# A fused scan and MLP on one core: the second product with stationary weights and its result turned back by VectorE

## The chip, the core and the metric

The kernel runs on one core of a Trainium2 chip. The metric is the device time in microseconds of one execution on that core, lower is better. A core has TensorE (PE, matrix products; PEld is its loading of stationary operands), VectorE (DVE), ScalarE (ACT), GpSimd (POOL) and SyncE (SP), which issues most of the DMAs here. The engines run their own instruction lists in order and wait for one another by semaphores. PSUM, where TensorE writes, has eight banks of 512 float32 columns.

## The reference

Two steps follow each other. The first is a chunked scan over 768 tokens for 4 batches x 8 heads (head size 32, state size 16); its result is regrouped into 3072 rows of 256. The second is an MLP with a hard-swish between two products (256 to 2048 to 256).

```python
for c in range(nc):                       # scan, per chunk
    cum = np.cumsum(la, axis=-1)
    L = np.exp(cum[:, :, :, None] - cum[:, :, None, :]) * causal
    CB = np.einsum('bhin,bhjn->bhij', Cc, Bc)
    y_intra = np.einsum('bhij,bhjd->bhid', CB * L, xc)
    y_inter = np.einsum('bhin,bhnd->bhid', Cc, state) * np.exp(cum)[:, :, :, None]
    y[:, :, sl] = y_intra + y_inter
    Bx = np.einsum('bhjn,bhjd->bhjnd', Bc, xc) * decay_from_j[:, :, :, None, None]
    state = decay_full[:, :, None, None] * state + np.sum(Bx, axis=2)
...
x = attn_out.transpose(0, 2, 1, 3).reshape(B * S, H * D)
h = x @ w_in                              # [3072, 256] @ [256, 2048]
g = h * np.clip(h + 3.0, 0.0, 6.0) / 6.0
out = g @ w_out                           # [3072, 2048] @ [2048, 256]
```

The inputs are float64 where the generator leaves them so; the kernel decodes the two weight matrices on the chip at the start. All products are float32.

## The kernel before

The work is cut into six blocks of 128 token positions; a block holds those positions of all four batches, so 512 rows of the MLP. The loop variable `k` is the block whose MLP runs, `c = k + 1` the block whose scan is woven into it, and `ahead = k + 2` the block that is prepared. No scheduler decides: the order of calls in the source is the order on each engine (`tc.manual_schedule()`).

A block's MLP in blocks 1 to 5 has two stages. In the first, eight steps `s` each make two hidden slices of 128 (f = 2s and 2s + 1) by a Strassen-Winograd scheme with seven half-size products: `lead` (two products, then a copy `even` <- `odd` on ScalarE, L667, and a copy `up` <- `odd` on VectorE, L668), `early` (two), `middle` (two, then the adds L680 and L681 on VectorE) and `last` (one). `ramp` (L688, ScalarE) and `times_ramp` (L693, VectorE) make the activated slices in `gT`. `g_sums` (L752, GpSimd) adds quarters of gT for the second stage.

The second stage is `out_units`. It is again a seven-product scheme, run once for each half t of the tokens of a quarter. Stationary operand is a 128 x 128 piece of gT (or of its sums), moving operand a 128 x 128 piece of the weights `w4` or of their sums `wsums`; the result comes out with tokens on partitions, in the banks `oa` and `ob`, and VectorE adds the parts into `res` (L791 to L813). Four DMAs per block (L816) store it, 128 rows of 1 KB each.

The generator yields after each product, and between its steps the loop issues the scan of the block `c`: after step 2 `scores` (its parts: `from_state` L500, the products `cb` L522 and `into_state` L534, into the banks f0 to f3, y0 and y1) and `multiply` (ScalarE's copy L550, VectorE's four products L563 of L with cb, in the middle of which `new_state` L544 makes `mid`), then `renew`; after steps 2 to 5 `decay_ends` for the block `ahead` (32 exponentials on ScalarE, L385, eight for each batch, and the `bs` products L396 on GpSimd); after step 6 `results` (`mix` L588 with `from_state`, `keep` L602 on ScalarE, `sum_y` L649 on VectorE), `from_start`, and `rows`, which issues the loads of L and eto on SP; after step 9 `turn_all` (VectorE transposes L465 and what follows), where the block ahead is 3 or later (`TURN` is 3); after step 12 the `lead` of the next block. `load(ahead)`, which loads B, C and x of a block on SP, is issued at the first step of a block's first stage.

Tiles of one tag share a bank or buffer in turn: `ps` has one buffer for each of the tags f0 to f3, `ps_o` two for the tag o, `ps_y` one for each of y0 and y1. A tile of a tag can be written only when the readers of the one before it are done.

Of the kernel before, what the change touches and what calls it, by code (L numbers as in the profile page):

```python
# [8 lines left out]
FP32 = mybir.dt.float32  # L9
# [4 lines left out]
ALU = mybir.AluOpType  # L14
# [6 lines left out]
def kernel(  # L21
# [24 lines left out]
    nc = tc.nc  # L46
    P = 128
    NB, NH, S, D = x.shape
    N = B.shape[-1]
    DM, DF = moe_w_in.shape[0], moe_w_out.shape[0]  # L50
    NC = S // P
    TB = NB * P
# [5 lines left out]
    HT = P // 2  # L58
# [7 lines left out]
    ffn = ctx.enter_context(tc.tile_pool(name="ffn", bufs=1))  # L66
    ps = ctx.enter_context(tc.tile_pool(name="ps", bufs=1, space=PSUM))
    ps_o = ctx.enter_context(tc.tile_pool(name="ps_o", bufs=2, space=PSUM))
# [14 lines left out]
    TURN = 3  # L83
# [71 lines left out]
    def conceal_in(t, pattern):  # L155
# [24 lines left out]
        out=head, in_=head, pattern=[[-2 * N, NQ], [-N, 2]], compare_op=ALU.is_ge,  # L180
        fill=0.0, base=0, channel_multiplier=1)
    nc.gpsimd.affine_select(
        out=head, in_=head, pattern=[[2 * N, NQ], [N, 2]], compare_op=ALU.is_ge,
# [140 lines left out]
    ys, cbs, sps, adds = {}, {}, {}, {}  # L324
# [177 lines left out]
                    rhs=csT[pair, b, HALF[a]], start=(a == 0 and b == 0), stop=True,  # L502
                    tile_position=(32 * q, d0), skip_group_check=True)

    def scores(c):

        bT, cT, _ = bTs[c]
        cbs[c] = [ps.tile([P, NB, 2, HT], FP32, name="cb", tag=f"f{q}") for q in range(NQ)]
        both = [ps_y.tile([P, 2, NB, HT], FP32, name=f"y{u}", tag=f"y{u}") for u in range(2)]
        ys[c] = {(0, u): both[u][:, 0] for u in range(2)}
        sps[c] = [both[a if c else 1 - a][:, 1] for a in range(2)]
        if c:
            from_state(c, 0)
        for b in range(NB):
            for a, rows in enumerate(HALF):
                for q in range(NQ):  # L520
                    pair = slice(32 * q, 32 * q + 32)
                    nc.tensor.matmul(  # L522
                        out=cbs[c][q][rows, b], lhsT=bT[pair, b, rows],
                        rhs=cT[pair, b, :, rows], start=(b == 0), stop=True,
                        tile_position=(32 * q, a * HT), skip_group_check=True)
        into_state(c, 0, 1)

    def into_state(c, *halves):
        xt, bs = xts[c], bss[c]
        for b in range(NB):  # L530
            for q in range(NQ):
                hs = slice(b * NH + 2 * q, b * NH + 2 * q + 2)
                for a in halves:
                    nc.tensor.matmul(  # L534
                        out=sps[c][a][32 * q:32 * q + 32, b],
                        lhsT=bs[HALF[a], hs].rearrange("s h n -> s (h n)"),
                        rhs=xt[HALF[a], hs].rearrange("s h d -> s (h d)"),
                        start=(c == 0 and b == 0), stop=True, tile_position=(a * HT, 32 * q),
                        skip_group_check=True)
# [34 lines left out]
            op=ALU.mult)  # L574
        new_state(states[c], adds[c], later)

    def mix(c):


        xt = xts[c]  # L580
        ys[c].update({
            (1, u): ps.tile([P, NB, HT], FP32, name="y2", tag=f"f{u}") for u in range(2)})
        for u in range(2):
            for b in range(NB):
                for h in range(u * HU, (u + 1) * HU):
                    for a, rows in enumerate(HALF):
                        d0 = D * (h % HU)
                        nc.tensor.matmul(  # L588
                            out=ys[c][a, u][d0:d0 + D, b], lhsT=xt[rows, b * NH + h],
                            rhs=Ls[c][rows, b, h], start=(b == 0 and a >= min(c, 1)), stop=True,  # L590
                            tile_position=(a * HT, d0), skip_group_check=True)
            if c == 0:
                from_state(c, 1, (2 * u, 2 * u + 1))
        if c:
            from_state(c, 1)

    def keep(c):
# [24 lines left out]
    NJ = NF // 2  # L622
# [97 lines left out]
    w4 = w_out.rearrange("p (j e) (m c) -> p e m j c", e=2, m=2)  # L720
    wsums = {}
# [15 lines left out]
    gsums = {}  # L737

    def g_quarter(k, e, r):
        return gTs[k].rearrange("p (j e) (r i) -> p e r j i", e=2, r=2)[:, e, r]  # L740
# [13 lines left out]
    def out_units(k):  # L754
# [15 lines left out]
        for t in range(2):  # L770
# [47 lines left out]
                    in_=res[:, 2 * r:2 * r + 2].rearrange("p m c -> p (m c)"))  # L818
            yield

    def rows(c):
        load_decay(c)
        load_eto(c)

    def results(c):
        mix(c)
        keep(c)
        sum_y(c)

# [4 lines left out]
    def load(c):  # L834
        load_bc(c)
        load_x(c)

    parts = {i: decode(i) for i in range(2 * NP)}

    def weights(i, n):  # L840
        for _ in range(n):
            next(parts[i], None)
# [62 lines left out]
    for k in range(NC):  # L905
        gTs[k] = ffn.tile([P, NF, TB], FP32, name="gT")
        c, ahead = k + 1, k + 2
        if k == 0:
            for f in range(NF):
                mlp_in(k, f)  # L910
                for i in weave.get(f, []):
                    weights(i, 1)
                if f in (6, 8):
                    diff_exp(c, f // 2 - 3)
            load(ahead)
            weights(NP + 1, 1)
            weights(NP + 3, 1)
            weights(NP + 2, 3)
            sums, sums_in = weight_sums(), in_weight_sums()
            for i in range(NP):  # L920
                for b in range(NB):
                    first_out(b, i, c)
                    if (i, b) == (0, 0):
                        weights(NP + 3, 1)
                        weights(NP + 2, 1)
                        weights(NP + 3, 3)
                        rows(ahead)
                    elif (i, b) == (1, 0):
                        next(sums_in)
                        next(sums_in)  # L930
                    elif (i, b) == (2, 0):
                        turn(c, 1)
                        wake(c)
                        turn(c, 0)
                        for p in range(2):
                            conceal(ahead, p)
                    elif (i, b) == (2, 3):
                        scores(c)
                        multiply(c)
                        renew(c)  # L940
                        decay_ends(ahead, 0)
                        decay_ends(ahead, 1)
                        next(sums)
                    elif (i, b) == (3, 0):
                        next(sums)
                        decay_ends(ahead, 2)
                    elif (i, b) == (3, 1):
                        results(c)
                        next(sums)
                        decay_ends(ahead, 3)  # L950
                    elif (i, b) == (3, 3):
                        from_start(ahead)
            rows(ahead + 1)
            continue
        for s in range(NJ):
            early(k, s)
            if s == 0:
                if ahead < NC:
                    load(ahead)
                if c < NC:  # L960
                    carry(c)
            if s < NJ - 1:
                lead(k, s + 1)
            if s:
                last(k, s - 1)
                ramp(k, 2 * s - 2, evens[k, s - 1])
            middle(k, s)
            if s:
                times_ramp(k, 2 * s - 2, evens[k, s - 1])
            ramp(k, 2 * s + 1, odds[k, s])  # L970
            times_ramp(k, 2 * s + 1, odds[k, s])
            if s in (1, 3) and ahead < NC:
                conceal(ahead, s // 2)
            if s in (3, 5) and c < TURN:
                turn(c, s // 4)
            if s in (2, 4, 6):
                g_sums(k, s - 2)
        for i, _ in enumerate(out_units(k)):
            if i == 0:
                s = NJ - 1  # L980
                last(k, s)
                ramp(k, 2 * s, evens[k, s])
                times_ramp(k, 2 * s, evens[k, s])
                g_sums(k, s - 1)
                if k == 1:
                    next(sums)
            if c < NC:
                if i == 2:
                    scores(c)
                    multiply(c)  # L990
                    if c < NC - 1:
                        renew(c)
                if ahead < NC and 2 <= i < 6:
                    decay_ends(ahead, i - 2)
                if i == 6:
                    results(c)
                    if ahead < NC:
                        from_start(ahead)
                    if ahead + 1 < NC:
                        rows(ahead + 1)  # L1000
                if i == 9 and TURN <= ahead < NC:
                    turn_all(ahead)
                if i == 12:
                    lead(c, 0)
# [30 lines left out]
```

## Time and profile before

| | us |
|---|---|
| median of three runs (lowest, highest) | 359.74 (359.16, 359.88) |
| the profiled execution, its own time | 359.64 |
| its span from first to last instruction | 357.9 |
| TensorE busy | 347.9 (97%) |
| VectorE busy | 221.9 (62%) |
| ScalarE busy | 177.5 (50%) |
| GpSimd busy | 137.9 (39%) |
| start of the `lead` of block 2, 3, 4, 5 in the chain | 139.34, 194.07, 248.79, 303.26 |

In the lines of the profile, a group has its place in the source (L766), its engine, operation, output <- input, shapes and count, then busy time. In a timeline or in the chain, the first number is the start in us from the start of the span, the second the length. "PE" lines are TensorE's passes; a float32 matmul appears as two of them. The granted TensorE clock was 0.995 of full speed on the mean.

### The profile page before, as it was taken

How to read it: one execution, taken by the hardware profiler on the slowest of the kernel's cores; microseconds unless marked ns; L12 is line 12 of the kernel's file. 1: busy time of each engine (PE TensorE's matmuls, PEld its weight loads, DVE VectorE, ACT ScalarE, POOL GpSimd, SP SyncE). 2: the span in 40 equal slices, each digit the busy share in tenths (PEclk: the TensorE clock that was granted, in tenths of full speed). 3: DMA queues.
4: the chain of work that ended last, by engine and by line, in shares of the span. 5: the costliest groups of instructions: out<-in, count | busy, mean ns of one | idle time of the engine just before them, and what ended most of it. 6: DMA issues, size and time to landing. Idle time of an engine off the chain costs nothing.

```text
span 357.9 us, 9350 instructions
## 1 busy us (share of the span) xinstructions
PE 347.9 (97%) x3936; PEld 300.0 (84%) x3936; DVE 221.9 (62%) x426; ACT 177.5 (50%) x390; POOL 137.9 (39%) x139
## 2 busy tenths in 40 slices
PE   5799999999999999999999999999999999999996
PEld 2554458888888999888999888999888999888996
DVE  6599999975887463686444687434587431588111
ACT  4678887267763730674650575560576010476100
POOL 3300000362599521099522089610068600058700
PEclk9899999999999999999999999999999999999999
DMA  8979969502924061550043560001000000000000
GB/s 166 201 277 185 266 165 127 116 4 84 155 57 60 5 136 58 81 80 2 4 113 82 74 88 2 4 2 35 26 2 1 4 3 31 29 3 0 2 29 31
DMA packets 75482, 24.97 MB, mean 70 GB/s; under 512 B 66032, under 2 KB 71824, under 8 KB 74928
## 3 DMA queue, kind: packets, MB, share of 16 engines
q1 hardware_dynamic: 71056, 23.06, 33.9%
q10 hardware_dynamic: 4384, 1.31, 1.7%
q8 instruction: 31, 0.51, 0.6%
q14 instruction: 11, 0.09, 0.1%
HBM read 21.07 MB, written 3.29 MB: 68 GB/s over the span
## 4 chain that ended last, share of the span: by engine, by line
PE 91%; DVE 3%; DMA 3%; ACT 1%; SPq 1%; issue 0%; DVEq 0%; ACTq 0%
PE ob L766 18%; PE even L652 18%; PE oa L766 18%; PE odd L652 13%; PE o L707 8%; PE h L610 8%; PE y L588 3%; PE y L500 2%; PE cb L522 2%; DMA raw<-in_moe_w_in_dram 2%; DMA pairs<-in_C_dram 1%; PE y L534 1%; SPq L100 1%; DVE odd L681 0%; DVE up L668 0%
## 5 line engine op out<-in xcount | busy, mean ns | idle before, releaser
L752 POOL TENSOR_TENSOR s<-gT 128x512 f32<-128x512 f32 x20 | 26.4, 1318 | 89.7 <-DVE gT L693 89.7
L652 PE MATMUL even<-ts,w_sum 128*128 128x256 f32 x160 | 48.2, 383 | 0.0
L667 ACT COPY even<-odd 128x512 f32<-128x512 f32 x40 | 23.0, 576 | 48.6 <-PE odd L652 46.3
L688 ACT ACTIVATE gT<-odd,half 128x512 f32<-128x512 f32 x40 | 27.5, 688 | 34.9 <-DVE odd L681 34.9
L652 PE MATMUL odd<-yT,w_in 128*128 128x256 f32 x160 | 41.1, 379 | 0.0
L766 PE MATMUL oa<-w_out,gT 128*128 128x128 f32 x320 | 38.9, 277 | 0.0
L766 PEld LDWEIGHTS oa<-w_out,gT 128*128 128x128 f32 x320 | 38.1, 192 | 0.9
L766 PE MATMUL ob<-w_out,s 128*128 128x128 f32 x320 | 37.4, 275 | 0.0
L766 PEld LDWEIGHTS ob<-w_out,s 128*128 128x128 f32 x320 | 36.5, 192 | 0.0
L652 PEld LDWEIGHTS even<-ts,w_sum 128*128 128x128 f32 x160 | 29.9, 190 | 5.3 <-ACT up L674 1.5
L693 DVE SCALAR_TENSOR_TENSOR gT<-gT,odd 128x512 f32<-128x512 f32 x40 | 27.5, 688 | 9.9 <-ACT gT L688 9.9
L652 PEld LDWEIGHTS odd<-yT,w_in 128*128 128x128 f32 x160 | 30.1, 190 | 3.9
L385 ACT ACTIVATE L<-L,cum_n 128x64 f32<-128x64 f32 x128 | 31.1, 339 | 0.0
L766 PE MATMUL ob<-t,gT 128*128 128x128 f32 x240 | 30.3, 279 | 0.0
L688 ACT ACTIVATE gT<-even,half 128x512 f32<-128x512 f32 x40 | 27.8, 695 | 4.4 <-PE even L652 4.4
L693 DVE SCALAR_TENSOR_TENSOR gT<-gT,even 128x512 f32<-128x512 f32 x40 | 27.2, 680 | 4.4 <-ACT gT L688 4.4
L766 PEld LDWEIGHTS ob<-t,gT 128*128 128x128 f32 x240 | 27.9, 192 | 1.2 <-issue 0.5
L707 PE MATMUL o<-w_out,gT 128*128 128x256 f32 x128 | 28.7, 381 | 0.0
L668 DVE COPY up<-odd 128x256 f32<-128x256 f32 x40 | 17.0, 424 | 18.6 <-ACT even L667 17.9
L610 PE MATMUL h<-yT,w_in 128*128 128x512 f32 x64 | 27.7, 594 | 0.0
L707 PEld LDWEIGHTS o<-w_out,gT 128*128 128x128 f32 x128 | 24.1, 190 | 3.7 <-issue 0.5
L563 DVE TENSOR_TENSOR L<-L,cb 128x512 f32<-128x512 f32 x24 | 15.3, 681 | 18.0 <-PE cb L522 15.5
(130 smaller groups left out, 609.8 us busy)
## 6 DMA issues: line engine op xcount, KB each, us to landing
raw<-in_moe_w_out_dram SPq DMA_DIRECT2D x4, 1024.0 KB
L<-cum_d SPq DMA_DIRECT2D x8, 512.0 KB
xt<-in_x_dram SPq DMA_DIRECT2D x6, 512.0 KB
raw<-in_moe_w_in_dram SPq DMA_DIRECT2D x3, 1024.0 KB
out_dram<-res SPq DMA_DIRECT2D x20, 128.0 KB
eto<-cum_e SPq DMA_DIRECT2D x20, 64.0 KB
B<-in_B_dram SPq DMA_DIRECT2D x5, 256.0 KB
raw<-in_moe_w_in_dram ACTq DMA_DIRECT2D x1, 1024.0 KB
```

Of the source, the lines that this page charges most:

```text
L385: nc.scalar.activation(Ls[c][:, b, h], Ls[c][:, b, h], AF.Exp, bias=cum_n[:, c, g:g + 1])
L563: nc.vector.tensor_tensor(out=Ls[c][:, :, hs], in0=Ls[c][:, :, hs], in1=cbs[c][q], op=ALU.mult)
L588: nc.tensor.matmul(out=ys[c][a, u][d0:d0 + D, b], lhsT=xt[rows, b * NH + h], rhs=Ls[c][rows, b, h], start=(b == 0 and a >= min(c, 1)), sto ...
L610: nc.tensor.matmul(out=h.rearrange("p r i -> p (r i)"), lhsT=w_in[:, j, f * P:(f + 1) * P], rhs=yTs[k][:, j].rearrange("p b i -> p (b i)") ...
L652: nc.tensor.matmul(out=bank[:, r], lhsT=lhsT, rhs=rhs, start=start, stop=True, skip_group_check=True)
L667: nc.scalar.copy(out=even, in_=odd[:, 1:2].to_broadcast([P, 2, 2 * P]))
L668: nc.vector.tensor_copy(out=up[:, 1], in_=odd[:, 0])
L688: nc.scalar.activation(gTs[k][:, f], h.rearrange("p r i -> p (r i)"), AF.Relu, bias=half, scale=1.0 / 6.0)
L693: nc.vector.scalar_tensor_tensor(out=g, in0=g, scalar=1.0, in1=h.rearrange("p r i -> p (r i)"), op0=ALU.min, op1=ALU.mult)
L707: nc.tensor.matmul(out=o[:, b % 2], lhsT=gTs[0][:, f, b * P:(b + 1) * P], rhs=w_out[:, f], start=(f == 0 and b % 2 == 0), stop=True, skip_ ...
L752: nc.gpsimd.tensor_tensor(out=o, in0=p_, in1=q_, op=op)
L766: nc.tensor.matmul(out=bank[:, slot], lhsT=lhs[:, j], rhs=rhs[:, j], start=(clear and j == 0), stop=True, skip_group_check=True)
```

## The change

In blocks 1 to 4 the second stage is made by a new generator, `wide_units`, while block 5 keeps `out_units` and block 0 its own form. The weights (or their sums) become the stationary operand, and a quarter of gT with 256 token columns is the moving one. A product is then eight matmuls of 256 columns, and there are seven products, each yielding twice, after four matmuls each. The result has output columns on partitions and tokens along the free dimension. VectorE transposes it in 32 x 32 squares (`turned_back`), and 32 DMAs per block store it, each 32 partitions of four runs of 32 floats.

The two `ps_o` banks `oa` and `ob` are taken once per block; a third bank, `oc`, is taken from tag f2 between the scan's use of that bank and the next block's. Two copies are made by ScalarE (`res`, `third`) and one by VectorE (`u2`).

The scan's parts move in two blocks. In block 2 (where c is TURN) `mix` issues its first half after step 6 and its second half after step 7, with `keep`, `sum_y` and what follows `results`. In block 4 (where c is NC - 1) `scores` leaves out `into_state`, which is issued after step 3, followed there by `multiply`.

```diff
-    def scores(c):
+    def scores(c, sums=True):
...
-        into_state(c, 0, 1)
+        if sums:
+            into_state(c, 0, 1)
...
-    def mix(c):
+    def mix(c, parts=range(2)):
...
-        for u in range(2):
+        for u in parts:
...
-        if c:
+        if c and 1 in parts:
             from_state(c, 1)
...
+    def wide_units(k):
+        halves = [[g_quarter(k, e, r) for r in range(2)] for e in range(2)]
+        g2, g4, g1 = (gsums[k][n] for n in (2, 4, 1))
+        def product(bank, slot, lhs, rhs, js, clear=False):
+            for j in js:
+                nc.tensor.matmul(
+                    out=bank[:, slot], lhsT=lhs[:, j], rhs=rhs[:, j],
+                    start=(clear and j == 0), stop=True, skip_group_check=True)
+        near, far = range(NJ // 2), range(NJ // 2, NJ)
+        res = ffn.tile([P, 2, 2, 2 * P], FP32, name="wide")
+        back = ffn.tile([P, 2, TB], FP32, name="back")
+        def turned_back(m, r=None):
...
+            nc.vector.transpose(out=o, in_=i)
+        def store(m):
+            for b in range(NB):
+                r0 = b * S + k * P
+                for q in range(4):
+                    c0 = m * P + 32 * q
+                    nc.sync.dma_start(
+                        out=out[r0:r0 + P, c0:c0 + 32].rearrange("(c i) m -> i c m", i=32),
+                        in_=back[32 * q:32 * q + 32, m, b * P:(b + 1) * P].rearrange(
+                            "i (c m) -> i c m", m=32))
+        oa, ob = (ps_o.tile([P, 2, 2 * P], FP32, name=n, tag="o") for n in ("wa", "wb"))
+        product(oa, 0, w4[:, 0, 0], halves[0][0], near, clear=True)
+        yield
+        product(oa, 0, w4[:, 0, 0], halves[0][0], far[:-1])
+        yield
+        product(ob, 0, wsums[4], halves[1][1], near, clear=True)
+        yield
+        product(ob, 0, wsums[4], halves[1][1], far)
+        yield
+        oc = ps.tile([P, 2, 2 * P], FP32, name="wc", tag="f2")
+        product(oc, 0, w4[:, 1, 0], halves[1][0], near, clear=True)
+        yield
+        product(oc, 0, w4[:, 1, 0], halves[1][0], far)
+        product(oa, 0, w4[:, 0, 0], halves[0][0], far[-1:])
+        nc.scalar.copy(out=res[:, 0, 0], in_=oc[:, 0])
+        nc.vector.tensor_tensor(out=res[:, 0, 0], in0=oa[:, 0], in1=res[:, 0, 0], op=ALU.add)
+        yield
+        product(oc, 1, wsums[3], halves[0][1], near)
+        yield
+        product(oc, 1, wsums[3], halves[0][1], far)
+        third, u2 = (ffn.tile([P, 1, 2 * P], FP32, name=n) for n in ("third", "u2"))
+        nc.scalar.copy(out=third, in_=oc[:, 1:2])
+        turned_back(0, 0)
+        yield
+        product(ob, 1, wsums[1], g1, near)
+        yield
+        product(ob, 1, wsums[1], g1, far)
+        nc.vector.tensor_tensor(
+            out=res[:, :, 1], in0=ob, in1=third.to_broadcast([P, 2, 2 * P]), op=ALU.add)
+        yield
+        product(oa, 0, wsums[2], g2, near)
+        yield
+        product(oa, 0, wsums[2], g2, far)
+        nc.vector.tensor_copy(out=u2, in_=oa[:, 0:1])
+        nc.vector.tensor_tensor(
+            out=res[:, :, 1], in0=res[:, :, 1], in1=u2.to_broadcast([P, 2, 2 * P]), op=ALU.add)
+        turned_back(0, 1)
+        store(0)
+        yield
+        product(ob, 1, w4[:, 1, 1], g4, near)
+        yield
+        product(ob, 1, w4[:, 1, 1], g4, far)
+        nc.vector.tensor_tensor(out=res[:, 1, 0], in0=ob[:, 1], in1=u2[:, 0], op=ALU.add)
+        turned_back(1)
+        store(1)
+        yield
...
-        for i, _ in enumerate(out_units(k)):
+        for i, _ in enumerate((wide_units if c < NC else out_units)(k)):
...
                 if i == 2:
-                    scores(c)
+                    scores(c, c < NC - 1)
+                if i == (2 if c < NC - 1 else 3):
+                    if i == 3:
+                        into_state(c, 0, 1)
                     multiply(c)
...
-                if i == 6:
-                    results(c)
+                if i == 6 and c == TURN:
+                    mix(c, (0,))
+                if i == (7 if c == TURN else 6):
+                    results(c, (1,) if c == TURN else range(2))
```

In the changed program, the lines after the new text move: L563 becomes L564, L668 L670, L680 L682, and the matmul of `product` is L832.

## The prediction

> **What bounds the kernel now.** I read the busy shares and the chain first, then the chain stage by stage in blocks 1 to 5 (blocks are k in the code; 0 is the first), then the timelines of the engines around each product stage.
>
> ```profile
> PE 347.9 (97%) x3936; PEld 300.0 (84%) x3936; DVE 221.9 (62%) x426; ACT 177.5 (50%) x390; POOL 137.9 (39%) x139
> PE 91%; DVE 3%; DMA 3%; ACT 1%; SPq 1%; issue 0%; DVEq 0%; ACTq 0%
> 153.28 1.29 PE even L652 x6
> ```
>
> TensorE is the bound: 97% busy, 91% of the chain. So only two things count: the rate of its passes, and what it waits for. The last line gives the rate of a pass that streams 256 columns: 1.29 / 6 = 0.2157 us (14 passes, 148.37 to 151.39 in the timeline, give the same). Each float32 matmul shows as two passes. This is the product stage of block 3 in the chain:
>
> ```profile
> 219.88 1.72 PE oa L766 x14
> 221.60 0.43 PE even L652 x2
> 222.04 3.79 PE oa L766 x34
> ...
> 227.43 0.79 PE y L534 x53
> 228.22 1.98 PE ob L766 x16
> 230.20 1.79 PE oa L766 x16
> 231.99 3.57 PE ob L766 x32
> ...
> 237.62 1.98 PE ob L766 x16
> 239.60 1.79 PE oa L766 x16
> 241.39 0.02 issue
> 241.41 2.02 PE ob L766 x16
> ```
>
> A pass of 128 columns is 3.57 / 32 = 0.1116 us. Where a group takes more, TensorE waited. The first 14 passes should take 1.56 and take 1.72: their last weights are gT of f = 12, which VectorE ends at 220.38 + 0.68 = 221.06. Each 1.98 is 0.19 over 1.79: it follows small-tile work (y, cb), and 0.19 is the price of one such visit, in and out. The 2.02 is 0.23 over: the second ob takes a bank that VectorE's L813 still reads, as this shows:
>
> ```profile
> 240.98 0.28 DVE L813 TENSOR_TENSOR res<-ob,u 128x128 f32<-128x128 f32 x1
> ...
> 241.38 1.86 PEld L766 LDWEIGHTS ob<-t,gT 128*128 128x128 f32 x16 [0.18 <-issue]
> ```
>
> The 2.02 is there in blocks 1 to 3, not in 4 (1.79 at 296.11).
>
> **The passes.** Before, a block's second product is 112 matmuls, 224 narrow passes: 224 x 0.1116 = 25.00. After, 7 products x 8 matmuls x 2 = 112 wide passes: 112 x 0.2157 = 24.16. Gain 0.84 per block; four blocks change (block 5 keeps the old form), so 3.36. Here a rule is to be weighed. TensorE: Matmul & The Clock Gate, section Back-to-back issue gap, says that in a stream of load-and-multiply pairs a 128-column matmul takes about 81 ns against 56 alone, so that loading costs some 25 ns each. The change drops 112 loads per block; at 25 ns this would be 11.2 us. The row decides: two narrow passes cost 223.2 ns, one wide 215.7, so a dropped load is worth 7.5 ns. Loads are hidden here.
>
> **Waits that go.** The 0.16 for f = 12: j = 6 now comes after 8 wide passes, the last even (0.43) and 4 more passes, 3.0 us in, not 1.3. Gain 0.16 in each of four blocks. The 0.23 for the ob bank: no second ob is taken. Gain 0.23 in blocks 1 to 3.
>
> **Waits that come.** I traced each bank through the instruction order of the changed program with its waits.
>
> (a) The first matmul of the product into slot 1 of the new bank oc is listed with a wait on ScalarE. The one ScalarE instruction it can be is the copy of oc slot 0: the bank is guarded as a whole. So a bank does wait for a copy, against the words of the change. And ScalarE's order puts that copy behind 24 of the 32 decay exponentials (blocks 1 to 3). Their rows:
>
> ```profile
> 228.28 0.37 ACT L550 COPY adds<-y 128x256 f32<-128x256 f32 x1 [2.04 <-PE y L534]
> 228.55 7.75 ACT L385 ACTIVATE L<-L,cum_n 128x64 f32<-128x64 f32 x32
> ```
>
> They start 0.33 after the end of into_state (228.22), at a pitch of (7.75 - 0.34) / 31 = 0.239. So the copy starts at +0.33 + 24 x 0.239 = +6.07, ends at +6.44 (0.37 as L550), and TensorE restarts at +6.60 (0.05 for the signal; 0.11 for an exposed load: the even at 218.20, held by DVE odd, lasts 0.70 where free ones last 0.59). Without it, TensorE would be there at 0.19 + 3 x 1.726 (8 passes each: ob far, oc near, oc far) + 0.43 = +5.80. Wait: 0.80 in each of blocks 1 to 3. Queued behind the copy are eight exponentials, then the copies of y; they have until the next block. In block 4 no exponentials run: the copy ends 0.41 after oc far, the two covering oa passes last 0.43, and 0.14 is left. Bounds for (a): 0.14 (ScalarE free) and 1.2 (one more copy-length late); I take 0.80, from the very rows.
>
> (b) oc needs the bank f2, which L563 for q = 2 reads. Blocks 1 to 3: cb ends at 227.43, and the second pair of L563 starts at 229.21, so q = 2 ends 229.21 + 0.68, 1.67 after into_state; TensorE comes at 0.19 + 1.73 = 1.92. No wait. In block 4, though, into_state is moved behind ob far, and VectorE's order is L, L, mid, mid, L, L with mid waiting for into_state. The rows of before, block 4:
>
> ```profile
> 282.21 1.28 DVE L563 TENSOR_TENSOR L<-L,cb 128x512 f32<-128x512 f32 x2 [4.01 <-PE cb L522]
> 283.42 0.60 DVE L544 SCALAR_TENSOR_TENSOR mid<-y,parity,tmp 128x128 f32<-128x128 f32 x2
> 283.94 1.27 DVE L563 TENSOR_TENSOR L<-L,cb 128x512 f32<-128x512 f32 x2
> ```
>
> Mid starts 0.07 after into_state, q = 2 ends 0.52 + 0.68 later, TensorE restarts 0.16 later: 1.43 during which it has nothing else. This is my value; ends 0.2 (a mere extra visit) and 1.7.
>
> (c) Block 2 splits mix around oc far: one more visit, 0.19 (ends 0 and 0.4, from the 1.98 rows). The steps of results move with its second part: the y copies, sum_y, from_start, and on SP two L and four eto loads. SP takes 1.85 + 2.50 for them in block 2 (182.37, 184.33); their readers are conceal (POOL) and carry in the next block, over 15 us later: nothing.
>
> (d) VectorE per block: out go L791 x2, L801, L802, L807, L811, L812, L813, 3.1 us; in come two adds of 256 (0.43 each), two of 512 (0.68), a copy (0.42), and transposes of 256, 256, 512. L465's row says 1.10 for 512; half for 256 is my estimate (0.55; ends 0.55 and 1.10). Sum 4.8, that is 1.7 more. ScalarE: two copies for one, 0.37. Neither bounds. What TensorE needs from them: the oa refill waits for an add done about 10 us before; the ob refill waits for the 512 add, done about 2.5 us before. At the block's end an add and the long transpose stand before L668, L680 and L681: see the rivals. Nothing.
>
> (e) Stores: 32 of 16 KB in 128-byte runs replace 4 per block. DMA: Bandwidth & Descriptors, Specifications, speaks against it: below 512 B a transfer is read, modified and written. Packets of this trace take 33.9% x 16 x 357.9 / 71056 = 27 ns, 4096 packets over 16 engines 7.0 us per block; doubled by the rule, 14 us. The DMA share is 0.33, 0.22 and 0.03 in blocks 2 to 4, so either fits. On SP:
>
> ```profile
> 204.20 4.54 SPq L100 DMA_DIRECT2D pairs<-in_B_dram  x8
> ```
>
> 0.57 each, 32 make 18 us. Behind them wait load(ahead): B, 16 pairs and x. B is then issued some 15 us later than at 197.59, its reader (bs, POOL) comes at 230.65 in block 3; the pairs' reader at 241.18. Cost nothing; no gain either, since no store is on the chain before block 5.
>
> **The sum.** Blocks 1 and 3: 0.84 + 0.16 + 0.23 - 0.80 = +0.43 each. Block 2: 0.43 - 0.19 = +0.24. Block 4: 0.84 + 0.16 - 0.14 - 1.43 = -0.57. Together 0.53 faster. Against the profiled execution, 359.64 (span 357.9 and 1.74 around it): 359.1. The median, 359.74, stands 0.10 above it, so 359.2.
>
> **Rivals.** A difference under 0.2% (0.72 us) can't be told from none here.
>
> 1. My sum, 359.2, with its small terms each off by 0.2: 358.6 to 359.8. Chance 0.55, of which 0.22 lie below 359.02.
> 2. The ScalarE wait is mostly not paid: with 0.14 instead of 0.80 in three blocks, 357.2. For it: before, ScalarE has idle time in this stage; against: the exponentials ran without a gap for 7.75. Chance 0.12.
> 3. Loads are worth the rule's 25 ns: 11.2 instead of 3.36, 351.4. Against: the 0.1116 row. 0.03.
> 4. The block's end becomes VectorE's. After the last product it has the 256 add (0.43) and the 512 transpose (1.10), 1.73 with the signal. L668 waits until 2.53 after that point today (253.81 against 251.28), L681 ends at 3.83, and TensorE needs it for the last even product at 4.38 (146.21 against 141.83 in block 2). So 0.8 + 0.5 = 1.3 us of slack. If the transpose or a late add eats more, TensorE waits in all four blocks: late by 1.75 us costs 0.45 each, 1.8 in all, and 361.0. It decides against the change (above 360.46) from 1.6 us on. For it: the slack is short; against: seven transposes in a narrow 1.08 to 1.11. 0.15.
> 5. The copy waits and visits are a little dearer and eat the gain: 359.7 to 360.6, 0.15.
>
> Faster 0.22 + 0.12 + 0.03 = 0.37; slower 0.15 + 0.03 of case 5's tail = 0.18; same 0.45. The range 357.8 to 360.8 leaves out case 3, most of 2 and the end of 4.
>
> **What would show it.** L832 at 0.2157 per pass; in blocks 1 to 3 a TensorE wait of about 0.8 on ScalarE's copy (L872) after the lone oa pass pair; in block 4 about 1.3 on L564 before the first oc pass; no wait at the ob refill; L668 and L682 no later against the first even product than now. A longer product stage in blocks 1 and 3, or a VectorE wait at a block's start, would prove me wrong.

## The result and the profile after

| | before | after |
|---|---|---|
| median of 22 runs each, us | 360.07 | 360.69 |
| profiled execution, its own time | 359.64 | 361.07 |
| its span | 357.9 | 359.3 |
| product stage of block 1, 2, 3, 4 | 29.13, 28.91, 28.91, 28.65 | 28.69, 29.05, 29.18, 30.22 |

The changed kernel takes 1.0023 of the time before, with an interval of 1.0001 to 1.0046; in a second comparison it took 1.0025 (1.0000 to 1.0051). That is some 0.8 us slower, where 0.5 us faster was forecast. (An execution's time goes with its mean granted clock, for the changed kernel 360.3 us at 0.997 or more, 361.6 at 0.99 and 364.9 at 0.98, and "at full clock" means those at 0.997 or more alone.) At full clock the difference is 0.9 to 1.2 us (before: 359.4 and 359.2 in two later comparisons), and between the two profiled executions it is 1.4. A product stage here runs from the first `oa` or `wa` of a block to the first product of the next block, in the chain; the half product that follows it takes 0.06 us less after, in every block. From here on, "the stage" means this.

The page of the changed kernel, first part and instruction refills (the queue's packets, MB, share):

```profile
PE 345.2 (96%) x3488; PEld 282.5 (79%) x3488; DVE 227.7 (63%) x426; ACT 178.7 (50%) x394; POOL 138.1 (38%) x139
q8 instruction: 27, 0.44, 0.5%
```

TensorE has 448 passes fewer and is busy 2.7 us less, and yet the span is 1.4 us longer: the difference is 4.1 us more of idle TensorE. The waits of TensorE say where (engine, line, what it waited for: us in total, times, longest):

```profile
PE wc L832 <- ACT wide L872: 1.9, 3, 0.6
PE wc L832 <- DVE L L564: 1.4, 1, 1.4
PE y L590 <- issue: 0.5, 2, 0.3
```

None of the three is in the list of before. The first two are the forecast ones, (a) and (b). The forecast had named 0.8 for each wait on L872, and 0.63 is listed; the other 0.24 of the cost is in the eight passes that follow each wait, which take 1.97 where eight undisturbed ones take 1.73. The third was not forecast: "issue" means that TensorE waited for nothing the profile shows, and L590 is `mix`. The chain of the changed kernel through the stage of block 3:

```profile
224.75 0.55 PE y L500 x25
225.37 0.98 PE cb L522 x55
226.35 0.83 PE y L535 x53
227.47 5.84 ACT L L385 x24
233.71 1.97 PE wc L832 x8
235.67 1.40 PE y L590 x89
237.56 0.62 PE y L500 x32
238.19 1.92 PE wc L832 x8
240.11 3.45 PE wb L832 x16
```

3.45 / 16 = 0.2157 us is the wide pass, as priced. From into_state's end the chain passes through 24 exponentials of ScalarE (L385) and on to the second `wc`. And `mix` (L590) has 1.89 us to the start of L500 (237.56 - 235.67), where in block 3 before it took 1.44 (235.56 to 237.00). The timeline of TensorE's passes there, and then that of its loads:

```profile
236.28 0.79 PE L590 MATMUL y<-L,xt 64*32 64x64 f32 x58
237.32 0.24 PE L590 MATMUL y<-L,xt 64*32 64x64 f32 x1 [0.26 <-issue]
237.49 0.69 PE L500 MATMUL y<-csT,mid 32*64 32x64 f32 x32
...
237.32 0.10 PEld L590 LDWEIGHTS y<-L,xt 64*32 64x32 f32 x1 [0.42 <-issue]
```

The very last of 128 small passes starts 0.46 us after the one before it, and its load is late too. Block 4, in the chain:

```profile
281.28 1.92 PE wb L832 x8
283.21 0.83 PE y L535 x53
284.10 0.61 DVE mid L545 x2
284.71 0.60 DVE L L564
285.44 3.69 PE wc L832 x16
289.69 1.97 PE wc L832 x8
291.65 1.07 PE y L590 x70
293.00 0.54 PE y L590 x35
293.54 0.62 PE y L500 x32
```

VectorE's `mid` waits for the moved `into_state`, L564 waits for `mid`, TensorE waits for L564: 1.40 us from 284.04 to 285.44. And `mix` pauses here too, between 70 and 35 recorded passes. The stage of block 3 is longer than before (29.18 against 28.91), which the prediction had named as a sign that it is wrong.

### The profile page after: what moved, and what is told of

It is laid out like the page before. It is cut to its first block, busy times and chain, and to the rows that moved or that the text cites. A ratio compares the mean times of both kernels' runs of the same rounds, so it can differ in the third digit from the quotient of the medians.

```text
span 359.3 us, 8565 instructions
## 1 busy us (share of the span) xinstructions
PE 345.2 (96%) x3488; PEld 282.5 (79%) x3488; DVE 227.7 (63%) x426; ACT 178.7 (50%) x394; POOL 138.1 (38%) x139
## 3 DMA queue, kind: packets, MB, share of 16 engines
q1 hardware_dynamic: 87184, 23.06, 35.5%
## 4 chain that ended last, share of the span: by engine, by line
PE 85%; ACT 6%; DVE 4%; DMA 3%; issue 1%; SPq 1%; DVEq 0%; ACTq 0%
PE even L654 18%; PE odd L654 13%; PE wb L832 10%; PE o L709 8%; PE h L612 8%; PE wa L832 7%; PE wc L832 5%; ACT L L385 5%; PE oa L768 4%; PE ob L768 3%; PE y L590 3%; PE cb L522 2%; PE y L500 2%; DMA raw<-in_moe_w_in_dram 2%; PE y L535 1%; DMA pairs<-in_C_dram 1%
## 5 line engine op out<-in xcount | busy, mean ns | idle before, releaser
L385 ACT ACTIVATE L<-L,cum_n 128x64 f32<-128x64 f32 x128 | 31.4, 339 | 0.0
L690 ACT ACTIVATE gT<-even,half 128x512 f32<-128x512 f32 x40 | 27.8, 695 | 4.4 <-PE even L654 4.4
L832 PE MATMUL wb<-s,w_out 128*128 128x256 f32 x128 | 29.7, 380 | 0.0
L403 POOL TENSOR_TENSOR tmp<-state,eto 128x256 f32<-128x256 f32 x5 | 3.4, 683 | 64.0 <-DMA eto<-cum_e 51.6
L670 DVE COPY up<-odd 128x256 f32<-128x256 f32 x40 | 17.0, 424 | 16.6 <-ACT even L669 15.7
L832 PEld LDWEIGHTS wb<-s,w_out 128*128 128x128 f32 x128 | 24.2, 190 | 3.3
L754 POOL TENSOR_TENSOR s<-s,gT 128x512 f32<-128x512 f32 x20 | 25.5, 1274 | 1.6
L754 POOL TENSOR_TENSOR gT<-gT 128x512 f32<-128x512 f32 x20 | 25.5, 1274 | 0.0
L754 POOL TENSOR_TENSOR s<-gT,s 128x512 f32<-128x512 f32 x20 | 25.4, 1272 | 0.0
L564 DVE TENSOR_TENSOR L<-L,cb 128x512 f32<-128x512 f32 x24 | 15.3, 680 | 14.9 <-PE cb L522 13.2
```

Of the source, the lines that this page charges most:

```text
L385: nc.scalar.activation(Ls[c][:, b, h], Ls[c][:, b, h], AF.Exp, bias=cum_n[:, c, g:g + 1])
L564: nc.vector.tensor_tensor(out=Ls[c][:, :, hs], in0=Ls[c][:, :, hs], in1=cbs[c][q], op=ALU.mult)
L670: nc.vector.tensor_copy(out=up[:, 1], in_=odd[:, 0])
L690: nc.scalar.activation(gTs[k][:, f], h.rearrange("p r i -> p (r i)"), AF.Relu, bias=half, scale=1.0 / 6.0)
L754: nc.gpsimd.tensor_tensor(out=o, in0=p_, in1=q_, op=op)
L832: nc.tensor.matmul(out=bank[:, slot], lhsT=lhs[:, j], rhs=rhs[:, j], start=(clear and j == 0), stop=True, skip_group_check=True)
```

## The experiments

**Pauses and refills.** The instruction queue q8 moves packets of 16 KB, 27 in this kernel, 31 before. TensorE's recorded instructions are 2 x 3488 (a load and a pass each): 6976 / 256 = 27.3, and before 7872 / 256 = 30.8. So q8 is taken for TensorE's list, one packet for 256 instructions. I numbered TensorE's loads and passes in each trace, and looked for the pauses that no wait explains and the packet that began before each. All pauses that no wait explains, from block 1 on and over 0.15 us, in five of the kernels (the last three are those of experiments 1, 3 and 5); the 0.19 that every start of `into_state` shows and the 0.13 that a block's first `wc` product loses, wherever they fall, are left out. Experiments 2 and 7 have no such pause.

| kernel | block, place | number of the instruction | above a multiple of 256 | us after a q8 packet began |
|---|---|---|---|---|
| before | 1, from_state | 2994 | 178 | 2.4 |
| after | 3, mix | 5038 | 174 | 2.4 |
| after | 4, mix | 6058 | 170 | 2.4 |
| scan undivided | 2, after from_state | 4016 | 176 | 2.4 |
| scan undivided | 3, mix | 5038 | 174 | 2.7 |
| scan undivided | 4, after into_state | 5804 | 172 | 2.8 |
| scan undivided | 4, mix | 6058 | 170 | 2.3 |
| both edits | 2, after from_state | 4018 | 178 | 2.4 |
| both edits | 4, after into_state | 5808 | 176 | 2.8 |
| both edits, shifted by 64 | 1, after from_state | 2996 | 180 | 2.4 |
| both edits, shifted by 64 | 3, after into_state | 4784 | 176 | 2.3 |

Every pause ends at the same place in a 256-instruction grid, and 2.3 to 2.8 us after a refill began. Block 0 has one more in some executions, at number 700, 188 above a multiple: none in the changed kernel's first profile, 0.91 us in its second, 0.75 in experiment 1. So whole times of one kernel can differ by nearly 1 us from this alone, and the stages are the finer measure. The clock is not behind the pauses: in all four stages of both kernels the granted clock is 1.00. Small-tile runs use up the list fastest: mix's 256 instructions take 1.44 us, in which wide passes use 13.

**1. The scan in one piece again.**

```diff
-                    scores(c, c < NC - 1)
-                if i == (2 if c < NC - 1 else 3):
-                    if i == 3:
-                        into_state(c, 0, 1)
+                    scores(c)
                     multiply(c)
...
-                if i == 6 and c == TURN:
-                    mix(c, (0,))
-                if i == (7 if c == TURN else 6):
-                    results(c, (1,) if c == TURN else range(2))
+                if i == 6:
+                    results(c)
```

> The changed kernel with the scan's parts in one piece again: in block 2 mix is issued whole after step 6, in block 4 scores issues into_state after step 2 and multiply follows there. Everything is computed. My account of the change (the division in block 4 costs the wait of TensorE for L564 of 1.40, an after-effect of about 0.08 and one more visit to small tiles of about 0.2; the one in block 2 costs a visit of about 0.2): 1.6 to 1.9 us less than the changed kernel, about 358.9 on the scale of its 360.69; the stage of block 4 falls from 32.81 to about 31.2 and that of block 2 from 31.64 to about 31.4. A pause marked issue inside mix may stay, move or go, since fewer visits change no count of instructions. Rival (the loss in block 4 is mostly supply of instructions in mix, and what waits for L564 would otherwise wait elsewhere): less than 0.7 us less, with the stage of block 4 above 32.2.

Measured: 362.72, ratio to before 1.0064 (1.0034 to 1.0095): slower than the changed kernel by some 1.5 us (0.0041 x 360; 1.3 at full clock, 0.8 in the stages), not faster by 1.6. Its stages: 28.70, 30.00, 29.45, 29.80. The waits of TensorE in its profile:

```profile
PE wc L832 <- ACT wide L872: 1.9, 3, 0.6
PE y L590 <- issue: 1.6, 3, 0.7
PE wc L832 <- issue: 1.3, 1, 1.3
PE wb L832 <- issue: 1.3, 1, 1.3
```

L564 is gone from the list, as expected. Of the 1.6 on L590, 0.75 is the pause of block 0 and the rest those in `mix` of blocks 3 and 4; the two of 1.3 are new. My account fell; the rival's numbers held. (They count the half product too: with its 2.59, block 4's 29.80 is 32.39, above 32.2.) The two pauses of 1.3 stand at the ends of the undivided small-tile runs: in block 2 after `mix` and `from_state`, in block 4 after `from_state`, `cb` and `into_state`. Block 2 in the chain:

```profile
180.61 1.41 PE y L590 x90
182.02 0.62 PE y L500 x32
182.64 1.33 issue
183.98 1.89 PE wc L832 x8
```

These are just the runs that the change divides. So the division isn't a pure cost: it puts eight wide passes, 1.73 us, into a run that would outrun its list.

**2. The products exchanged.** The product of `g1` goes before the second one into `oc`, so that TensorE has 16 wide passes (3.45 us) beside ScalarE's copy.

```diff
-        product(oc, 1, wsums[3], halves[0][1], near)
-        yield
-        product(oc, 1, wsums[3], halves[0][1], far)
...
-        turned_back(0, 0)
-        yield
         product(ob, 1, wsums[1], g1, near)
         yield
         product(ob, 1, wsums[1], g1, far)
+        turned_back(0, 0)
+        yield
+        product(oc, 1, wsums[3], halves[0][1], near)
+        yield
+        product(oc, 1, wsums[3], halves[0][1], far)
...
```

> The changed kernel with two products of the second stage exchanged: g1 with wsums[1] into slot 1 of ob comes before the second product into oc, so that ScalarE's copy of oc slot 0 has 3.45 us of TensorE work beside it. Everything is computed, with the same count of instructions. My account (the wait of the second oc product for the copy behind the exponentials is 0.80 in each of blocks 1 to 3 and 0.29 in block 4): 2.4 to 2.8 us less than the changed kernel, no TensorE wait on L872 or its successor. Rival 1 (the same bank or the copy of the third sum is then late for the following product, a new wait): less than 1 us less, and a new wait for ScalarE or VectorE of 0.5 or more at the next ob or oa product. Rival 2 (TensorE was not really held there, the exponentials set no end): no change.

Measured: 357.18, ratio to before 0.9924 (0.9890 to 0.9958), 3.5 us less than the changed kernel. Stages 27.81, 28.19, 27.83, 29.39, that is 0.88, 0.86, 1.35 and 0.83 below the changed kernel's. In block 3 the first `wc` product, the covering passes and `wb` now follow one another:

```profile
228.15 3.58 PE wc L832 x16
232.16 1.73 PE wb L832 x8
233.89 1.41 PE y L590 x90
```

The wait for L872 is gone and no other has come; (a) is shown. It gave more than expected because the pauses in mix of blocks 3 and 4 went with it. The traces hold a reason: in all five profiles in which block 3 has both the copy wait and the pause (the changed kernel's two, the undivided one, and two with few stores), the refill that the pause hung on began 1.15 to 1.25 us after TensorE went on from that wait; here, with no wait, the packet ahead of the same instruction began 5.6 us before it, where the changed kernel has 2.4. So TensorE's wait may hold back the order for its own next refill. No run separates this from other causes, and it is not general: in the L564 wait of block 4 a refill began 0.9 us before the wait's end in three profiles (experiment 6).

**3. Both edits.**

> Both edits together on the changed kernel: products exchanged, scan in one piece. Everything is computed. If the two costs are separate and add up, 4.0 to 4.6 us less than the changed kernel, that is about 3.5 to 4.0 less than the kernel before (ratio to before 0.989 to 0.991). If they share a cause (a common later wait, for example VectorE at the end of the block), the sum falls short by more than 1 us and a VectorE wait shows at the first even product of the next block.

Measured: 356.79, ratio 0.9894 (0.9850 to 0.9938); 3.9 us less than the changed kernel, 0.1 short of what was expected. But by stages, 27.81, 28.99, 27.83, 28.71, the gain is not the expected one: blocks 1 and 3 are clean, and 2 and 4 pause:

```profile
PE wb L832 <- issue: 1.7, 2, 1.0
```

Against experiment 2, undividing mix in block 2 costs 0.80, and undividing scores in block 4 gains 0.68, since it takes away the L564 wait and brings a pause of 0.73.

**4. A shift of TensorE's list by 128.** 64 tiny matmuls with one pass each, ahead of the first block's scores.

```diff
     weights(0, 1)
+    more = ps.tile([P, NH, HT], FP32, name="d", tag="f3")
+    for i in range(64):
+        nc.tensor.matmul(
+            out=more[HALF[i % 2], 0], lhsT=pick[:, :1].to_broadcast([P, HT]),
+            rhs=split[:, 1, HALF[i % 2]], start=True, stop=True,
+            tile_position=(0, i % 2 * HT), skip_group_check=True)
     scores(0)
```

> The changed kernel with 64 tiny matmuls more (128 instructions on TensorE) issued before the first block's scores, where TensorE is idle, into a bank that is cleared later. Nothing else differs. Theory that the pauses marked issue inside mix of blocks 3 and 4 (0.26 on the matmul side and about 0.45 in length each) come from where the refills of TensorE's instruction list fall, 256 instructions at a time: the pauses leave those two places or change size there, and may appear at others; the length of mix in blocks 3 and 4 goes from 1.89 to about 1.44, the whole time by -0.9 to +0.5. Rival (they come from the data, that is from L, x or a bank being late in those blocks): both pauses stay, 1.89 each, the whole time unchanged within 0.3 us.

Measured: 369.46, ratio 1.0232 (1.0177 to 1.0287), far outside what was expected. The chain at the start:

```profile
18.50 2.81 issue
21.31 1.13 PE d L490 x2
...
25.54 1.26 issue
```

Two pauses, ending at 188 and 186 above a multiple of 256, cost 4.1 us ahead of block 0's `h`; another 2.2 us are in the 64 passes of block 0's `h` (29.84 against 27.66), where the granted clock is 0.7 in the two slices up to 36.9 us. Neither was foreseen, and both lie outside the changed stages. In the stages the question is answered: 29.28, 29.08, 28.70, 31.64. The pause of block 3 is gone; in block 4 it has left mix and stands, now 1.57 us, in the `from_state` behind it, at number 6314, 170 above. One of about 0.45 came in block 1 (number 2996, 180 above) and one of 0.50 in block 2 (3762, 178 above). The same data, other places: the rival (late data) is out. And block 3 with its copy wait but without a pause takes 28.70.

**5. A shift by 64, in the kernel with both edits.** A block has 1088 = 4 x 256 + 64 of these instructions, so 64 more should give each block the pattern of the next.

```diff
             early(k, s)
+            if k == 1 and s == 3:
+                for j in range(2):
+                    more = ps_o.tile([P, 2, 2 * P], FP32, name="more", tag="o")
+                    for i in range(8):
+                        nc.tensor.matmul(
+                            out=more[HALF[i % 2], 0, :HT], lhsT=ident[:, :HT],
+                            rhs=ident[:, :HT], start=(i < 2), stop=True,
+                            tile_position=(0, i % 2 * HT), skip_group_check=True)
```

> The kernel with both edits (products exchanged, scan in one piece), and in the first stage of block 1, after step 3's early, 16 tiny float32 matmuls more: 32 passes, so 64 instructions on TensorE, into a bank that is cleared later; they cost about 0.36 + 0.19 = 0.55 us themselves. In all six kernels so far a pause marked issue ended at an instruction whose number, counted over TensorE's loads and passes, is 170 to 180 above a multiple of 256, and a block has 1088 = 4 x 256 + 64 of them. If refills of 256 instructions are the cause, 64 more give each block the pattern that the next one had: the pauses of 1.00 and 0.73 in blocks 2 and 4 leave them and appear, 0.7 to 1.3 long, in blocks 1 and 3, at the same places of the stage (after the second from_state in 1, after into_state in 3); the stages from 27.81, 28.99, 27.83, 28.71 to about 28.8, 27.8, 28.7, 27.7, and the whole time within 0.8 us of that kernel plus 0.55. Rival (the pauses come from what blocks 2 and 4 do, such as the loads of the block ahead or its decay ends): they stay in blocks 2 and 4 and the four stages stay as they were.

Measured: stages 28.79, 27.82, 27.97, 27.83, against 27.81, 28.99, 27.83, 28.71 without the shift. The pauses left blocks 2 and 4 and came in 1 and 3; that of block 1 in TensorE's timeline, ahead of the third wide pass of `wb`, where block 2 had it ahead of the second:

```profile
127.95 0.69 PE L500 MATMUL y<-csT,mid 32*64 32x64 f32 x32
128.57 0.70 PE L832 MATMUL wb<-s,w_out 128*128 128x256 f32 x2
129.97 1.56 PE L832 MATMUL wb<-s,w_out 128*128 128x256 f32 x6 [0.70 <-issue]
```

Block 3's was small, 0.14 in the stage where 0.7 or more was expected. The whole time, 358.37, is 1.0 above the sum expected, and 0.8 was allowed. Half of that is the tiny matmuls, which took 1.08 us, 34 ns a pass and not 11; the rest does not show in the profiled executions, whose spans are 355.7 and, without the shift, 355.5. The sizes were thus not foreseen, but the places were: that they move with the count of instructions, from block to block as computed, shows the refills as the cause of the pauses.

**6. Few stores and transposes.** Two of three transposes and 30 of 32 stores of each changed stage are left out.

```diff
-            nc.vector.transpose(out=o, in_=i)
+            if r == 0:
+                nc.vector.transpose(out=o, in_=i)
...
-                for q in range(4):
+                for q in range(1 if m == 0 and b < 2 else 0):
```

> The changed kernel with two of the three VectorE transposes of each product stage and 30 of its 32 stores left out (most of the rows of blocks 1 to 4 are then not written). TensorE's instructions are untouched. My account (d and e of the prediction: transposes and stores lie beside other work and cost nothing): the whole time within 0.4 us of the changed kernel, the four product stages at 28.69, 29.05, 29.18 and 30.22 (first wa to the next block's first product) each within 0.1, and the pauses marked issue in mix of blocks 3 and 4 in place. Rival 1 (VectorE at the end of a block holds TensorE a little): 0.3 to 0.6 less in each of four blocks, 1.2 to 2.4 in all. Rival 2 (the 128 stores on the DMA engines slow the refills of TensorE's instructions): the two pauses of 0.45 shrink or go, 0.9 less.

Measured: stages 28.69, 29.05, 29.20, 29.75; whole time 361.52, ratio 1.0046 (1.0004 to 1.0088). Blocks 1 to 3 are unmoved: transposes and stores cost nothing there. The whole time is 0.8 above the changed kernel's, where 0.4 was allowed; at full clock the two have 360.0 and 360.3. In block 4 the pause was missing, 0.47 less. To tell chance from stores, the changed kernel and this one ran once more:

> The changed kernel once more, nothing edited, for the pause in mix of block 4 (0.45 in its first profile, absent where stores and transposes were left out). If the length of a pause depends on when the refill of TensorE's instructions happens to be served, it may be missing or of another size here too, in block 3 or 4, with the stages of blocks 1 and 2 at 28.69 and 29.05 within 0.1. If the stores cause it, both pauses are here again at 0.45.

> The same again with two of three transposes and 30 of 32 stores of each product stage left out (most rows of blocks 1 to 4 unwritten). If stores cause block 4's pause, it is absent here again (stage 29.75) while it is there in the changed kernel's own second profile. If its length is chance, it may be here too (30.2).

Measured: 360.76 for the changed kernel, stages 28.70, 29.06, 29.50, 29.75; with few stores 361.61, ratio 1.0021 (0.9982 to 1.0060), stages 28.70, 29.19, 29.39, 29.75. So block 4's pause is missing in the changed kernel itself, and block 3's is larger: the sizes change from one execution to the next, with the stores and without. Where the pause was missing, in three profiles, a refill began 0.9 us before the end of the L564 wait; where it was there, the same refill (the 23rd packet of the queue) came only at 290.65, after the copy wait.

**7. A better version.** Products exchanged, mix divided in block 2 as in the change, and in block 4 `from_state` alone half a product earlier, with `cb`, `into_state` and `multiply` together, so that `mid` no longer waits. `begin` takes the banks of scores, `square` is its `cb` and `into_state`.

```diff
+                if i == 1 and c == NC - 1:
+                    begin(c)
+                    from_state(c, 0)
                 if i == 2:
-                    scores(c, c < NC - 1)
-                if i == (2 if c < NC - 1 else 3):
-                    if i == 3:
-                        into_state(c, 0, 1)
+                    if c < NC - 1:
+                        scores(c)
+                    else:
+                        square(c)
                     multiply(c)
```

> The changed kernel with the products exchanged; mix stays divided in block 2; in block 4 scores is divided elsewhere: from_state alone is issued one product half earlier (after step 1), cb, into_state and multiply together after step 2. So VectorE's mid no longer waits for a late into_state, and TensorE has eight wide passes (1.73 us) between from_state and cb in which a refill can land. Everything is computed. Theory (the division helps because it spreads the small tiles over a refill, and it hurts only through the L564 wait): stages 27.8, 28.2, 27.8 and about 28.0, no pause marked issue over 0.2 in blocks 1 to 4, 1.2 to 1.6 us less than with products exchanged alone, about 355.7 (ratio to before 0.983 to 0.990). Rival (the division in block 4 has nothing to do with refills, the pause after into_state comes there anyway): a pause of 0.7 to 1.3 after into_state in block 4, stage 28.7 or more, at most 0.7 us less. A third way: the wait for L564 persists because VectorE is late for other reasons: 29.2 or more in block 4.

Measured: 356.27, ratio to before 0.9905 (0.9889 to 0.9922), about 0.9 us less than with the exchange alone by the medians, 1.2 by the stages and 1.5 at full clock (two executions against seven); 1.2 to 1.6 was expected. Stages 27.82, 28.19, 27.83, 28.18, where 27.8, 28.2, 27.8 and 28.0 were expected. Block 4 in the chain of this kernel (its lines stand a little lower: L836 is L832 of the changed one):

```profile
275.07 0.62 PE y L500 x32
275.69 1.92 PE wb L836 x8
277.62 1.14 PE cb L527 x63
278.75 0.79 PE y L539 x53
279.54 1.92 PE wb L836 x8
281.46 3.58 PE wc L836 x16
```

`wc` follows `wb` without a gap: no wait for L564, and no pause after `into_state`. Experiment 3 has a median only 0.5 us above this one; by its stages this version is 1.3 us shorter (112.02 against 113.34).

## Why the prediction was wrong

The sum was to be -0.53 over the four blocks. The stages and the half products after them give 28.69 + 29.05 + 29.18 + 30.22 - (29.13 + 28.91 + 28.91 + 28.65) - 4 x 0.06 = +1.30: off by 1.83. (This is the pair of profiled executions; the changed kernel's second profile gives +1.17.) Step by step, with the clean stage of experiments 2, 3 and 7, 27.82, as the rod:

- **The passes and the waits that go** (0.84, 0.16, 0.23): right within 0.1. An undisturbed stage of before has 28.91; less 0.78 (0.84 without the half product's 0.06) and 0.39 that would be 27.74, and it is 27.82: 0.08 too hopeful, and 0.11 in block 4 (28.65, where the 0.23 is not due), 0.35 in all; the first `wc` after a visit takes 3.58 where sixteen passes take 3.45, which is of that size. The row was a better guide than the Trainium skill's page TensorE: Matmul & The Clock Gate, section Back-to-back issue gap: loads worth 25 ns would have given 11.2 us, and were not there to win.
- **(a), the copy behind the exponentials**, 0.80: the wait was right, 28.69 - 27.81 = 0.88 in block 1. In block 4 it was put at 0.14 and is 0.36 (29.75 in the second profile, against 29.39 with the exchange). The wait itself is 0.13 there (289.69 against 289.13 + 0.43); the other 0.24 is again the slow start of the eight passes behind it. Over the four blocks 0.43 short (0.08, 0.06, 0.07, 0.22).
- **(b), L564 in block 4**, 1.43: the wait itself, 1.40, was right. With it comes a visit that this term left out: 29.39 - 27.81 = 1.58, 0.15 short.
- **(c), the price of a visit**, "0.19 in and out": it is 28.19 - 27.82 = 0.37 in block 2, and the same in block 4 of experiment 7 (28.18). The 0.19 of the 1.98 rows was the way out alone. Halving mix shows the way in: 0.79 + 0.79 where the whole takes 1.41. 0.18 short. (The rows stand below the list.)
- **What was not in the sum at all: TensorE's instruction supply.** Before loses about 0.22 to it in block 1 (29.13 against 28.91); the changed kernel loses 0.48 in block 3 (29.18 against 28.70, which is 27.83 and block 1's copy wait) and 0.47 in block 4. Net 0.48 + 0.47 - 0.22 = 0.73, the largest piece of the miss.

The halves of mix, block 2 of the changed kernel in the chain:

```profile
180.86 0.79 PE y L590 x53
181.65 1.92 PE wc L832 x8
183.57 0.79 PE y L590 x53
```

Pieces: 0.35 + 0.43 + 0.15 + 0.18 + 0.73 = 1.84, to be set beside 1.83. So the mechanisms of (a) and (b) were right and their sizes short, the price in (c) was half of what a visit costs, and one mechanism was missing. Without the pauses the forecast would still have been some 1.1 off, with +0.6 in place of -0.5. The failed steps, in the prediction's words, are "one more visit, 0.19" in (c), "0.14 is left" in (a), and the sum, which has no term for a pause. Term (c) also priced the division of mix as a cost alone, with nothing against it: with the products exchanged it is worth 0.80 in block 2 (experiment 3 against 2), and 0.95 in the order of the change (experiment 1). Rival 5 had dearer visits and copy waits and gave them 359.7 to 360.6, that is 0 to 0.9 us slower than before; the 0.8 measured lies in that, but dearer visits and waits are only 0.76 of the 1.84 (0.43, 0.15 and 0.18).

A page of the Trainium skill would have warned of the mechanism, though not of the cost: Runtime: NRT & Kernel Launch, section Instruction fetch mechanics, says that an engine's instructions come in blocks of 16 KiB, 256 instructions each, over a DMA queue that the sequencer drives, and that crossing a boundary is mostly hidden because instructions are issued slower than they arrive. The trace agrees on the 256 and the 16 KB. It disagrees on "hidden": mix issues 256 instructions in 1.44 us, 5.6 ns each, a packet takes 0.9 to 1.9 us of transfer alone, and pauses of up to 1.33 us followed in experiment 1.

**(d) and (e)** were right: three of four stages did not move when most transposes and stores were left out. VectorE is even less loaded than I put it: what comes in sums to 4.2 us a block, not 4.8. The groups of VectorE in the changed kernel:

```profile
L465 DVE STREAM_TRANSPOSE csT<-pairs 128x512 f32<-128x512 f32 x4 | 4.4, 1103 | 2.9 <-DMA pairs<-in_C_dram 2.9
L846 DVE STREAM_TRANSPOSE back<-wide 128x256 f32<-128x256 f32 x8 | 3.6, 444 | 0.2
L846 DVE STREAM_TRANSPOSE back<-wide 128x512 f32<-128x512 f32 x4 | 2.8, 711 | 0.1
```

I took 1.10 for the long one from L465; it takes 0.71. So rival 4, the block's end becoming VectorE's, had no chance: the copy L670 (L668 before) starts at 253.70 in block 3's end, where before it started at 253.81. The short runs of the stores, against which the skill's page DMA: Bandwidth & Descriptors, section Specifications, speaks, cost nothing either; they lie beside other work. The doubling of their time to 14 us was my own reading of that page's read-modify-write and does not show: all packets of the queue took 35.5% x 16 x 359.3 = 2041 us against 33.9% x 16 x 357.9 = 1941, so 1.6 us more per DMA engine and changed block, the old stores' time already taken off.

What stays open: what orders a refill when (it began some 1.2 us after a wait's end in some profiles and well ahead in others), and why block 4's pause comes in one execution and not in the next.

## What to carry to other kernels

Price a change of the matmul engine's list also by how fast it runs through its instructions: a run of some 250 small-tile instructions without a wide pass among them can outrun its refills, as here, and then a wide product put in the middle gains more than the visit costs. Where the chain shows "issue" on TensorE, number its instructions and look at the grid of 256 before blaming data. And where a bank waits for a copy that stands behind a queue of other work, exchange the order of products before anything else: here that alone made some 0.9 us in each of blocks 1 to 3 and took two pauses with it.

## What was unexpected of the hardware

- Pauses of TensorE of 0.2 to 2.8 us at one place of a grid of 256 instructions (170 to 188 above a multiple), where small tiles (11 ns a pass) stand ahead of it; adding 128 tiny instructions at the start of a 360 us kernel made it 8.8 us longer, of which 4.1 are two pauses.
- The pauses' sizes change between executions of one kernel: block 4's was 0.47 in one and none in another, block 3's stage 29.18 and 29.50.
- A visit of small tiles amid wide passes costs 0.37 us, half on the way in.
- A 32 x 32 square transpose of 128 x 512 takes 0.71 us here and 1.10 in L465, same shape and type; its source and destination differ, and no run was made on why.
